# Linear attention beside a squared-ReLU MLP on one core: queries in the Strassen loop, a transposed second MLP product, and weight operands streamed from DRAM

## The chip, the cores and the metric

The kernel runs on one core of a Trainium2 chip. The metric is the device time of one execution in microseconds, from the first to the last thing that the core does. Before the change it is 423.73 us, the median of three runs (423.67 to 424.07).

## The reference

The input x has 2048 tokens of 512 numbers. All numbers are 32-bit floats. The output is x plus two branches that read the same normalised tokens:

```python
xn = layernorm(x)                                  # 2048 x 512
# branch A: linear attention, 32 heads of 16
q, k, v = split(xn @ wqkv)                         # wqkv 512 x 1536
phi = lambda t: where(t > 0, t + 1, exp(t)) + 1e-6
kv  = phi(k)^T @ v  (16 x 16 per head);  z = sum over tokens of phi(k)
o   = (phi(q) @ kv) / (phi(q) . z + 1e-6)
A   = o @ wo                                       # wo 512 x 512
# branch B: MLP
h   = relu(xn @ w1 + b1) ** 2                      # w1 512 x 1376
B   = h @ w2 + b2                                  # w2 1376 x 512
out = x + A + B
```

## The kernel before, in words

Tokens come in 16 tiles of 128 and four blocks of four tiles (512 tokens). `NF` = 11 chunks of 128 columns make up w1; the last has 96 and carries the bias b2 as an extra row, so `NP` = 5 pairs of whole chunks remain. Every large operand is kept as a high and a low part in a rounded 32-bit format (`split`, line 114: ScalarE copies the high part, VectorE subtracts it from the source for the low part). A product of two split operands is three passes (high·high, high·low, low·high; `three`, line 124), each a matmul with a 128x128 stationary operand and 512 columns moving.

The work goes in this order. First come the statistics and the normalisation. Then a loop over the 16 tiles (line 612 on) computes keys (`project`, line 329), their phi (`phi_k`, line 342) and `kx`, the product of phi(k) with the tokens (line 346, four accumulators). In that loop `pieces` (line 603) converts weights that are needed later. After it, `values` and `matrix` (lines 727 and 742) fold kv and wo into one 512x512 matrix m that is kept in SBUF.

The main loop `for n in range(2)` (line 750) takes two blocks at a time, t1 and t2. In it:

- `queries` (line 357) computes q of one tile with 12 matmuls and `phi`; `attention` (line 365) multiplies by z, sums over the 16 columns of a head, takes the reciprocal and scales; `regroup_q` and `attention_T` turn the result by DMA moves and VectorE transposes.
- The loop over `p` (line 869) computes the hidden columns of one pair of w1 chunks for both blocks by the Strassen-Winograd scheme: seven `product` calls (line 420) of six matmuls each instead of eight. The sums of w1 chunks (`chunk_sums`, line 656) and their parts (`chunk_split`) are made on chip in `aop`, right before they are used, and again for each n. The sums of tokens are in `T`.
- `mlp_2` (line 428) multiplies the hidden columns (stationary) with a chunk of w2 (moving, in `w2r`, made by `piece_2`, line 192): 12 matmuls for one chunk and four tiles. For t1 it runs inside the loop over p, for t2 after it (line 994 on), where `add_attention` (line 432) adds the attention product.
- The tokens-by-columns result gets x added by one VectorE instruction a tile (`add`, line 861) and leaves by one DMA a tile (`store`, line 865). The last tile is done in two halves of 256 columns (`end`).

Order and resources: this is a manual schedule; each engine runs its instructions in the order in which the program writes them. All DMAs are issued by the SP queue, in program order too: a DMA that must wait holds up those behind it. PSUM has two sets of four banks, `ps` and `acc`, which take turns. The instruction names in the profile are the tile names with numbers left out: `acc` for the second product, `b` for the Strassen products, `pk`, `pq` and `kx` for keys, queries and the token product.

## Time and profile before

| | before |
|---|---|
| median of three runs | 423.73 us |
| span of the profiled execution (first to last instruction) | 422.3 us |
| what lies around the span | 1.4 us |
| TensorE matmul, busy | 417.5 us (99%) |
| VectorE, busy | 298.8 us (71%) |
| ScalarE, busy | 248.4 us (59%) |
| GpSimd, busy | 28.7 us (7%) |
| bytes moved by DMA | 43.02 MB, mean 102 GB/s |
| granted TensorE clock | 1.00 all the way |

The profile is of one execution. It gives each engine's busy time, the chain of work that ended last, groups of like instructions with count and mean duration, and tables by stretches of time. Matmuls are pipelined, so the mean duration of one is longer than the distance between two. "PEld" is the loading of stationary operands, beside the matmuls.

### The profile page before, as it was taken

To read this page: it belongs to the slowest core of one execution; us is meant where nothing else is said; L and a number is where in the kernel's file an instruction comes from. 1 tells how busy PE (TensorE), PEld (TensorE's weight loads), DVE (VectorE), ACT (ScalarE), POOL (GpSimd) and SP (SyncE) were. 2 spreads that over 40 slices of the span, in tenths; PEclk is the share of its full clock that TensorE was granted. 3 is DMA by queue.
4 is the path that set the end of the run, shared out by engine and by line. 5 is a ranking of instruction groups with operands and counts; after the bars stand their busy time and mean duration, and the time that the engine had idled before them with its cause. 6 is when DMAs were issued, how large, how long until landed. Compare 5 with 4: busy or idle time off the path is not lost.

```text
span 422.3 us, 5369 instructions
## 1 busy us (share of the span) xinstructions
PE 417.5 (99%) x1868; PEld 345.2 (82%) x1868; DVE 298.8 (71%) x537; ACT 248.4 (59%) x441; POOL 28.7 (7%) x50
## 2 busy tenths in 40 slices
PE   8999999999999999999999999999999999999996
PEld 7788888888887888888888888888888888888885
DVE  6897788855668886777579376586977668577353
ACT  5766667644467777566467353666667665556240
POOL 2242222230000000000000000000000000000000
PEclk9999999999999999999999999999999999999999
DMA  7863437000412321646016752501120654024502
GB/s 236 281 168 83 107 102 223 25 0 2 112 50 58 93 72 54 185 87 177 0 54 203 185 201 76 144 0 50 51 75 25 200 98 152 1 87 95 162 0 99
DMA packets 42754, 43.02 MB, mean 102 GB/s; under 512 B 5828, under 2 KB 28612, under 8 KB 42472
## 3 DMA queue, kind: packets, MB, share of 16 engines
q1 hardware_dynamic: 42728, 42.69, 34.5%
q8 instruction: 14, 0.23, 0.3%
q14 instruction: 12, 0.10, 0.1%
HBM read 30.09 MB, written 6.29 MB: 86 GB/s over the span
## 4 chain that ended last, share of the span: by engine, by line
PE 99%; DVE 0%; issue 0%
PE acc L127 38%; PE b L424 23%; PE pk L332 10%; PE kx L351 10%; PE pq L332 10%; PE pz L127 1%; PE b L127 1%; PE warm L464 1%; PE pt L275 1%; PE pkv L733 1%; PE pm L127 1%; PE end L127 0%; DVE zb L439 0%; DVE res L863 0%; DVE eps L440 0%
## 5 line engine op out<-in xcount | busy, mean ns | idle before, releaser
L127 PE MATMUL acc<-w2r,s 128*128 128x512 f32 x498 | 116.6, 389 | 0.0
L127 PEld LDWEIGHTS acc<-w2r,s 128*128 128x128 f32 x498 | 93.5, 188 | 19.6
L424 PE MATMUL b<-T,aop 128*128 128x512 f32 x240 | 59.6, 389 | 0.0
L424 PEld LDWEIGHTS b<-T,aop 128*128 128x128 f32 x240 | 45.0, 188 | 9.4
L351 PE MATMUL kx<-pk,tok 128*128 128x512 f32 x192 | 47.0, 394 | 0.0
L351 PEld LDWEIGHTS kx<-pk,tok 128*128 128x128 f32 x192 | 35.5, 188 | 7.8 <-DVE pk L340 0.5
L127 PE MATMUL acc<-mh,aTsr 128*128 128x512 f32 x96 | 30.3, 390 | 0.0
L108 ACT ACTIVATE w2r<-r 128x512 fp32r<-128x512 f32 x32 | 20.0, 625 | 13.6 <-PE acc L127 11.3
L119 DVE TENSOR_TENSOR w2r<-r,w2r 128x512 fp32r<-128x512 f32 x32 | 21.9, 685 | 7.3 <-ACT w2r L108 7.2
L424 PE MATMUL b<-xs0h,aop 128*128 128x512 f32 x80 | 26.4, 391 | 0.0
L116 POOL TENSOR_TENSOR tok<-xp,tok 128x512 fp32r<-128x512 f32 x16 | 22.4, 1402 | 53.5 <-ACT tok L108 53.5
L116 DVE TENSOR_TENSOR s<-c,s 128x512 fp32r<-128x512 f32 x20 | 13.8, 692 | 16.7 <-ACT s L108 16.7
L327 DVE SCALAR_TENSOR_TENSOR q<-pq,q 128x512 f32<-128x512 f32 x16 | 11.0, 689 | 16.7 <-ACT q L325 16.7
L108 ACT ACTIVATE aop<-S 128x512 fp32r<-128x512 f32 x20 | 12.6, 629 | 14.7 <-DVE S L662 9.4
L127 PEld LDWEIGHTS acc<-mh,aTsr 128*128 128x128 f32 x96 | 18.0, 188 | 3.8
L863 DVE TENSOR_TENSOR res<-acc,res 128x512 f32<-128x512 f32 x16 | 11.0, 692 | 14.0 <-PE acc L127 13.9
L198 POOL MEMSET r<- 32x512 f32 x3 | 1.6, 522 | 278.3 <-DVE w2r L119 278.3
L323 ACT ACTIVATE q<-pq 128x512 f32<-128x512 f32 x16 | 9.5, 591 | 18.4 <-PE pq L332 18.4
L323 ACT ACTIVATE k<-pk 128x512 f32<-128x512 f32 x16 | 9.5, 594 | 17.0 <-PE pk L332 16.8
L127 PE MATMUL acc<-ml,aTsr 128*128 128x512 f32 x48 | 18.7, 390 | 0.0
L424 PEld LDWEIGHTS b<-xs0h,aop 128*128 128x128 f32 x80 | 15.0, 188 | 3.4 <-ACT rz L412 0.3
L424 PE MATMUL b<-xs0l,aop 128*128 128x512 f32 x40 | 15.6, 389 | 0.0
(188 smaller groups left out, 831.4 us busy)
## 6 DMA issues: line engine op xcount, KB each, us to landing
r<-in_B_w_dram SPq DMA_DIRECT2D x49, 256.0 KB, 3.2
res<-in_A_x_dram SPq DMA_DIRECT2D x8, 512.0 KB, 6.0
g<-q SPq DMA_DIRECT2D x64, 64.0 KB, 2.1
out_dram<-res SPq DMA_DIRECT2D x15, 256.0 KB, 2.0
x<-in_A_x_dram SPq DMA_DIRECT2D x5, 512.0 KB, 4.3
xTd<-t SPq DMA_DIRECT2D x8, 256.0 KB, 3.1
rq<-in_A_wqkv_dram SPq DMA_DIRECT2D x8, 256.0 KB, 5.8
xg<-xp SPq DMA_DIRECT2D x32, 64.0 KB, 2.0
```

The source lines that it names most:

```text
L108: nc.scalar.activation(o, i, AF.Copy, bias=bias)
L116: ENG[el].tensor_tensor(out=l, in0=src, in1=f32(h), op=OP.subtract)
L119: nc.vector.tensor_tensor(out=l, in0=src, in1=f32(h), op=OP.subtract)
L127: nc.tensor.matmul(ps, lhsT=a[u], rhs=b[v], start=first and n == 0, stop=last and n == 2)
L275: nc.tensor.transpose(p[:, at_j], xp[i][:, at_j], ident)
L323: nc.scalar.activation(p, ps, AF.Relu, scale=-1.0)
L327: nc.vector.scalar_tensor_tensor(p, ps, 0.0, p, op0=OP.max, op1=OP.add)
L332: nc.tensor.matmul(ps, lhsT=cols(i)[u][:, j, slot(i)], rhs=w[v][:, j, :], start=first and n == 0, stop=last and n == len(steps) - 1)
L351: nc.tensor.matmul(kxp[c], lhsT=tok[i][:, u, c * P:(c + 1) * P], rhs=pk[i][:, v], start=i == 0 and (u, v) == first, stop=i == NT - 1 and ( ...
L424: nc.tensor.matmul(ps, lhsT=a[u][:, j * P:(j + 1) * P], rhs=b[v][:, j, :], start=first and j == 0 and n == 0, stop=last and j == 1 and n == 2,
L464: nc.tensor.matmul(pw[:, :P], lhsT=zb[:, :P], rhs=zb[:, :P], start=True, stop=True)
L863: nc.vector.tensor_tensor(out=r[:, a:z], in0=ps, in1=r[:, a:z], op=OP.add)
```

## The change

The change rewrites the main loop.

- Queries no longer run tile by tile. The four chunks of wq become `NQ` = 2 pairs at the head of the Strassen loop, so the loop has `NK` = 7 pairs; a pair's outputs are transposed (columns on partitions). phi (`phi_1`) and the shares of a head (`shares`: one ScalarE activation with scale and bias, VectorE transposes, a reduction over 32-wide blocks, reciprocal, transpose back, scale) work on that form. `attention`, `regroup_q` and `attention_T` are gone.
- The second MLP product is transposed: the weights are stationary and the hidden columns move (`second`: six matmuls with two stationary 128-column halves and three passes into two banks). For the first two blocks (n = 0) it has as many matmuls as before; for the last two (n = 1) pairs of w2 chunks and the two blocks are multiplied with seven products (`combinations` makes the sums of hidden columns, `prepare_t` those of w2).
- Every stationary operand of the loop is a 256 KB block [128, 512] that is prepared once (`prepare_1`, `prepare_2`, `prepare_t`, `prepare_z`: load, sum, split into a staging tile, `spill` to DRAM in `wd1`, `wd2`, `wdz`) and read back when it is used: `fetch_ops` keeps eight slots filled in the order `order_of` gives; `used` frees a slot after its six matmuls and issues the next fetch. `m` goes to DRAM (`wdm`) and is prepared like a w2 chunk.
- A table `PLAN` says at which of six places of a pair a preparation step ("p"), a share step ("l"), a token sum ("s") or a combination ("c") is issued.
- Results are transposed, so each goes through a VectorE transpose and an addition to x (`add_turned`); x is loaded and the output stored in blocks of 32 partitions with rows of 64 numbers, 256 bytes (`out_blocks`, `load_res`, `store`): 32 loads and 32 stores of 128 KB.

The diff, cut to its core (n = 1 and the preparation of w2 look alike):

```diff
-    def mlp_2(acc, f, s, first=False):
-        for k in range(TB):
-            three(acc[k], [s[:, u, k * P:(k + 1) * P] for u in range(2)], w2s[f], first, False)
+    def fetch_ops():
+        while order and op_turn[1] < len(op_slots) and order[0] in ready:
+            key = order.pop(0)
+            t = op_slots[op_turn[0] % 8]
+            nc.sync.dma_start(f32(t), place_of(*key))
+            loaded.append((key, t))
+            op_turn[0] += 1
+            op_turn[1] += 1
+    def used(n=1):
+        op_turn[1] -= n
+        fetch_ops()
+    def product(ps, key, b, first=False, last=False):
+        a = op(*key)
+        for j in range(2):
+            for n, (u, v) in enumerate(PASSES):
+                nc.tensor.matmul(ps, lhsT=a[:, u * 256 + j * P:u * 256 + (j + 1) * P], rhs=b[v][:, j, :], ...)
+        used()
+    def second(ps, key, s, first=False, last=False):
+        a = op(*key)
+        for n, (u, v) in enumerate(ORDER):
+            for c in range(2):
+                nc.tensor.matmul(ps[c], lhsT=a[:, u * 256 + c * P:u * 256 + (c + 1) * P], rhs=s[:, v], ...)
+        used()
+    def ops_of(kind, k, i, src, el="dve"):
+        n = src.shape[1]
+        t = stage()[:, :n]
...
+        split(o[:, 0], o[:, 1], src, "act", el)
+        spill(kind, k, i, t)
+    def prepare_1(k, el="dve"):
...
+        return [lambda: ops_of("1", k, 0, ra, el), sums_12, sums_34, lambda: ops_of("1", k, 6, rb[:, 1:], el)]
+    def add_turned(r, c, src):
+        o = w512("o", "d", 2)
+        nc.vector.transpose(o, src)
+        at = r[:, :, c // 2].rearrange("p b (d c) -> p b c d", c=2)[:, :, c % 2]
+        nc.vector.tensor_tensor(out=at, in0=o.rearrange("p (b d) -> p b d", d=32), in1=at, op=OP.add)
+    PLAN = ((("s", "s", "p", "p", "p", "p"), ("p",) * 6, ("p",) * 6, *[("pl", "l", "p", "p", "pl", "pl")] * 4, ("", "l", "l")),
+            (("", "", "", "", "", ""), ("", "l", "", "p", "p", ""), *[("l", "l", "p", "l", "c", "l")] * 2,
+             *[("p", "l", "c", "p", "cl", "p")] * 3, ("l", "c", "c")))
-        for p in range(NP + 1):
+        for p in range(NK + 1):
...
+                product(A, ("1", p, 0), [x[:, :2] for x in x1], True)
...
+            if f_before:
+                add_product(p - 1, 0)
+            if p:
+                product(before, ("1", p - 1, 6), [T[4][:, u] for u in range(2)], False, True)
+                finish(p - 1, 1, before)
...
+            product(A, ("1", p, 3), [T[2][:, u] for u in range(2)])
+            copy("act", R[2], A, one)
+            hook(plan.pop(0))
+            product(C, ("1", p, 5), [x[:, 2:] for x in x2], False, True)
...
+            if f_before:
+                add_product(p - 1, 1)
...
+            product(A, ("1", p, 4), [T[3][:, u] for u in range(2)])
+            if n == 0 and p == 3:
+                for b in (t1 - 2, t2 - 2):
+                    nc.sync.dma_start(xT[b], xTd[b])
+            if p == NK - 1:
+                res = {t1: load_res(t1, "W0" if n else "r3")}
...
+        jobs += attentions([*V, *W], 2, True, False)
+        at_end(lambda: (add_to(o["m5"], W), turned_to(t2, 2, o["m5"]), store(res[t2], t2, 1)))
+        jobs += phase_jobs(V, 7, False, True)
+        at_end(lambda: (turned_to(t2, 0, V), store(res[t2], t2, 0)))
```

More of the change, by code (lines that the diff above doesn't have):

```diff
@@ L79, in w512 @@
         return work.tile([P, 512], F32, name=name, tag=tag, bufs=bufs)
-    turns = {"x": [0, 2], "pair": [0, 5]}
+    turns = {"x": [0, 2], "pair": [0, 5], "raw": [0, 4], "st": [0, 4]}
     def next_tag(of):
@@ L407, in hidden_2, with second_z, parts_of @@
+    def second_z(ps, cs, s, first=False, last=False):
+        a = [op("z", 0, 2 + u) for u in range(2)]
+        for n, (u, v) in enumerate(ORDER):
+            for b, c in zip(ps, cs):
+                nc.tensor.matmul(b, lhsT=a[u][:, c * P:(c + 1) * P], rhs=s[:, v],
+                                 start=first and n == 0, stop=last and n == 2, skip_group_check=True)
+        used(2)
+    def parts_of(name, src):
         s = pair(name)
-        split(s[:, 0], s[:, 1], r, "act", "dve")
+        split(s[:, 0], s[:, 1], src, "act", "dve")
@@ L1025 @@
[L1025 to L1045 removed]
+                finish(p - 1, 3, t5)
```

874 lines of the change are left out of this document (453 added, 421 removed).

## Prediction, written before the changed kernel ran

> **What bounds the kernel now.** First the page's head: busy shares, the slices and the DMA queue.
>
> ```profile
> span 422.3 us, 5369 instructions
> ...
> PE 417.5 (99%) x1868; PEld 345.2 (82%) x1868; DVE 298.8 (71%) x537; ACT 248.4 (59%) x441; POOL 28.7 (7%) x50
> ...
> DMA  7863437000412321646016752501120654024502
> GB/s 236 281 168 83 107 102 223 25 0 2 112 50 58 93 72 54 185 87 177 0 54 203 185 201 76 144 0 50 51 75 25 200 98 152 1 87 95 162 0 99
> ...
> q1 hardware_dynamic: 42728, 42.69, 34.5%
> ```
>
> TensorE is busy in 99%; the DMA engines only in 34.5%, in bursts. A busy PE may still be waiting inside its pipeline, so I read the distance between matmuls next: the chain that ended last, and one stretch of the main loop from the table of windows.
>
> ```profile
> PE 99%; DVE 0%; issue 0%
> ...
> 207.80 54.60 PE acc L127 x240
> ```
>
> ```profile
> 300.00:315.00 15.00, 15.00 (x68) 12.43 (x67) 11.71 (x22) 10.26 (x18) 0.00 (x0) 1.00 0.24 69
> ```
>
> The chain is one row of matmuls; 240 of them take 54.60 us, 0.227 us each, at clock 1.00. So the matmul count sets the time, and a 512-column matmul is worth 0.227 us. In a Strassen stage of 15.00 us VectorE works 11.71 and ScalarE 10.26 us: both have room, neither has much.
>
> **TensorE's part.** The queries were 16 x 12 = 192 matmuls; as two pairs for two block pairs they are 2 x 2 x 7 x 6 = 168. The second product of the last blocks was 10 chunks x 8 tiles x 3 = 240; with seven products it is 5 x 7 x 6 = 210. All else keeps its count. 54 matmuls go: 54 x 0.227 = **-12.3 us**, if none of the rest waits. What the change brings onto the other engines decides.
>
> **DMA.** Each block of 256 KB feeds six matmuls, so the loop must take 262 KB every 6 x 0.227 = 1.36 us, and the blocks must have been written before. By the code the kernel moves 117 MB instead of 42.7. What does a full DMA move?
>
> ```profile
> 3.00:6.00 3.00, 3.00 (x16) 3.00 (x16) 2.17 (x8) 1.07 (x5) 0.00 (x0) 1.00 1.00 346
> 71.00:74.00 3.00, 3.00 (x15) 2.46 (x15) 3.00 (x4) 2.05 (x4) 0.83 (x2) 1.00 0.93 311
> 220.00:225.00 5.00, 5.00 (x24) 4.13 (x23) 4.86 (x10) 1.38 (x3) 0.00 (x0) 1.00 0.90 345
> 266.50:269.00 2.50, 2.50 (x12) 2.07 (x12) 1.33 (x2) 1.73 (x3) 0.00 (x0) 1.00 0.97 252
> ```
>
> The last two columns are DMA share and GB/s. Loads in rows of 2 KB give 346 at a full share (and 311/0.93 = 334); a mix of an 8 KB-row load with 2 KB-row stores gives 345/0.90 = 383; loads of w1 columns, 512-byte rows, 252/0.97 = 260.
>
> n = 0 is where blocks are both made and used. Counting the SP queue's DMAs of the changed kernel between the end of pair 0 and the end of pair 5, in blocks of 262 KB: 47 operand fetches (7 + 7 + 11 + 11 + 11), 50 spilled, 15 raw w2, wo-product and bias rows, 6 of w1, 4 of m, 8 of xT: 130 blocks, 34.1 MB. Transfer time: the 6 blocks of w1 1.6 MB / 260 = 6.0 us; the other 32.5 MB 84.8 us at 383, 93.9 at 346. TensorE needs for these five pairs 47 x 1.36 + 12 x 0.227 (m) = 66.7 us. The excess is 24 to 33 us. It can't be put off, since the SP queue is one line: a fetch stands behind the spills issued before it. Only the look-ahead covers some: eight slots are 10.9 us, less the landing of one.
>
> ```profile
> r<-in_B_w_dram SPq DMA_DIRECT2D x49, 256.0 KB, 3.2
> ...
> out_dram<-res SPq DMA_DIRECT2D x15, 256.0 KB, 2.0
> ...
> out_dram<-res SPq DMA_DIRECT2D x2, 128.0 KB, 1.7
> ```
>
> A block lands in 3.2 us, so 10.9 - 3.2, about 8 us, is cover. The wait is 16 to 25 us. I take **+16**: the traffic is a mix of stores and loads, as in the row that gives 383. The low end for the range is 0, should stores and loads together run well over the 383 of this trace.
> The Trainium skill (HBM Reference, Access; DMA: Bandwidth & Descriptors, Bandwidth) has a core streaming alone at about 425 GB/s; no full stretch here reaches it. By that the 32.5 MB take 76.5 us and the wait is 8 us instead of 16.
>
> In the other stages the stream fits: pair 6 has 4.5 MB in 15 us, the n = 1 loop's full pairs 9 fetches, 4 spilled and 2 raw blocks, 3.9 MB in 12.3 us (320 GB/s).
>
> The residual loads are in 256-byte rows, which this trace doesn't have: 1 MB for each block, two blocks nearly at once at the end of each loop. Bounds: at the 260 of 512-byte rows 2.1 MB take 8 us, at half of it 16. Operands in hand and issued between them cover 13 x 1.36 = 17.7 us in n = 0, ten (13.6 us) in n = 1; with the fetches between (3.5 and 1.4 us) and 3.2 us of landing the wait is 0 to 5 and 0 to 7. I take **+3** together.
> The Trainium skill's DMA page (Specifications) puts the smallest transfer at line rate at 512 bytes; no row here is under it, and by that rule the half rate, 16 us, is the likelier end, which would make +3 into +12 (5 and 7).
>
> **VectorE and ScalarE.**
>
> ```profile
> L116 DVE TENSOR_TENSOR s<-c,s 128x512 fp32r<-128x512 f32 x20 | 13.8, 692 | 16.7 <-ACT s L108 16.7
> ...
> L371 DVE TENSOR_REDUCE den<-pz 128x32 f32<-128x512 f32 x16 | 11.0, 686 | 0.6
> ...
> L261 DVE STREAM_TRANSPOSE at<-g 128x512 f32<-128x512 f32 x16 | 10.5, 690 | 7.1 <-DMA g<-q 7.1
> ...
> L373 DVE RECIPROCAL den<-den 128x32 f32<-128x32 f32 x16 | 5.7, 353 | 0.6
> ...
> L662 DVE TENSOR_TENSOR S<-S,r 128x256 f32<-128x256 f32 x10 | 4.2, 425 | 0.3
> ```
>
> ```profile
> 8.70 0.68 DVE L487 TENSOR_TENSOR wkl<-rk,wkh 128x512 fp32r<-128x512 f32 x1
> 9.30 0.68 DVE L293 TENSOR_TENSOR xs1l<-pt,xs1h 128x512 fp32r<-128x512 f32 x1
> ```
>
> A 512-wide instruction takes 0.69 us, but the next can start 0.60 us later (8.70, 9.30). Those are the two ends. A full pair of n = 0 has 17 such, 5 of 256 and 2 reciprocals: 17 x 0.69 + 5 x 0.42 + 0.7 = 14.5 us in 15.0 (11 x 1.36): the DMA wait hides it. In n = 1 a full pair has 9 x 1.36 = 12.3 us of TensorE, and VectorE 16 x 0.69 + 6 x 0.42 + 0.35 = 13.9 us, 11.9 by the closer spacing; for the two heaviest pairs 0 to 3.2 us over. I take **+2**.
>
> At the end of that loop VectorE has ten instructions left (six sums of hidden columns among them) and then the low part for the first job: 11 x 0.60 to 0.69 = 6.6 to 7.6 us, while TensorE has two operands and four matmuls, 3.6 us: **+3**. Later, at three borders of the n = 1 sums, six VectorE instructions (3.6 to 4.1 us) and a split (0.69) stand before the third job's low part, which TensorE wants after the same 3.6 us: 0.7 to 1.2 each, **+2**.
> The short chain of a pair, from the A22 product over relu, square and high part on ScalarE to the second product, is three ScalarE instructions of 0.63 to 0.69 and has two operands (2.7 us) to hide in: nothing, at most 0.6 a pair if ScalarE is behind, 6 in all. A full pair of n = 0 gives ScalarE 18 instructions, 11.5 us of 15.
>
> **The tail.**
>
> ```profile
> 417.47 1.59 PE L127 MATMUL end<-w2r,s 128*128 128x256 f32 x12
> ...
> 419.10 0.42 DVE L863 TENSOR_TENSOR res<-end,res 128x256 f32<-128x256 f32 x1 [0.29 <-PE end L127]
> ```
>
> ```profile
> 36.61 10.11 SPq L257 DMA_DIRECT2D xg<-xp x16
> ```
>
> Now TensorE ends at 419.06 and the span at 422.3, 3.2 us later: half an addition and one small store. After the change both banks of the last sum end together: two transposes and two additions (4 x 0.60 + 0.1 = 2.5 us), then four stores, issued 0.63 us apart (10.11 us for 16), so the last 1.9 us after the first, then the 2.8 us that stand now behind the last addition, and 0 to 2 more for 256-byte rows. 7.2 to 9.2 us against 3.2: **+5**.
>
> **Sum.** 422.3 - 12.3 + 16 + 3 + 2 + 3 + 2 + 5 = 441.0; the 1.4 us around the span (423.73 less 422.3) make **442 us**, slower by 4%.
>
> **Rivals.**
> 1. *The transfers keep up*: stores and loads together pass the 383 and the waits shrink to what the look-ahead covers. Then -12.3, the tail +4 to +5, and 0 to 4 for VectorE: 415 to 421, faster. For it: stretches of a full DMA with mixed traffic are few here and short. Against it: it needs 34.1 MB in 66.7 + 8 us, 456 GB/s, over every row above. Chance 0.17.
> 2. *Partly*: 430 GB/s in the mix; the wait is 32.5/0.43 + 6.0 - 66.7 - 8 = 7 us, the rest at its low ends (+9): 423.7 - 12.3 + 16 = 427. Chance 0.15.
> 3. *The preparations come late as well*: in the full queue a raw row lands behind eight others (8 x 262 to 524 KB, 6 to 11 us), ScalarE, in order, waits for it at the split, and with it the copies that TensorE needs, so a fetch that has landed doesn't help. It decides as soon as a step is asked for less than such a time after its load was issued; a step is asked for every 2.5 to 3 us and at most three are held. One such wait of 2 to 4 us in each of five pairs: 452 to 462. Chance 0.22.
> 4. *The cut does not show*, because the second product gains nothing per matmul from going in two banks by turns: for 0.01 us more on 690 matmuls, +7. The present second product changes its stationary operand with every matmul too and runs at 0.227, so 0.02, together with no change at all.
>
> The forecast, 430 to 451, has 0.44. The range: rival 1 at its lower end and rival 3 at its upper: **415 to 462**, which leaves out some 0.15. Faster by over 0.2% 0.18, within 0.2% (about what a measurement can tell) 0.03, slower 0.79.
>
> **What the profile will show.** Right: 1722 matmuls of 512 columns at 0.227 where nothing waits; DMA slices of 9 tenths and 340 to 400 GB/s from the first pairs to the fifth of n = 0, with TensorE waiting there for operand blocks and nearly nowhere else; a gap of about 3 us after the n = 1 loop; 7 to 9 us from the last matmul to the end. Wrong: DMA shares below 0.9 in n = 0 while TensorE waits (then the queue's order or a split is the wait, not the rate); rates over 420 there; waits in n = 1 that sum to more than 15 us.

## The result, and the profile after

The changed kernel takes **515.39 us** (median of four runs, 511.4 to 518.54) against 423.7 for the kernel before: ratio 1.216, 95% interval [1.210, 1.222]. Slower was foretold, but by 4%, not by 22%, and 515 lies far outside the range of 415 to 462. The profiled execution took 518.5 us, the longest of the four; its span is 516.4.

The page's head of the changed kernel: the span, TensorE's busy time, the slices of the granted clock and of the DMA engines, the queue, and the chain that ended last by engine.

```profile
span 516.4 us, 5845 instructions
...
PE 443.2 (86%) x1808; PEld 346.0 (67%) x1808; DVE 331.0 (64%) x551; ACT 255.6 (49%) x438; POOL 28.1 (5%) x48
...
PEclk9999899999888897999879999989989898799998
DMA  7834556556899899999976877776447749956853
...
q1 hardware_dynamic: 96868, 117.09, 73.0%
...
DVE 31%; PE 28%; ACT 16%; DMA 12%; issue 7%; SPq 4%; DVEq 0%; ACTq 0%
```

The chain was 99% TensorE; now VectorE leads with 31%, although VectorE is busy in only 64% of the span. No engine is full. The matmuls became fewer and TensorE's busy time grew from 417.5 to 443.2 us: some of them ran at nearly half rate (in the timeline of pair 5 of n = 1 six take 2.90 us at 403.83 and 1.52 at 390.26). The DMA is at 8 or 9 tenths throughout in slices 11 to 20 alone (12.9 us each): the n = 0 loop.

So I went by stage. A **pair** is here what lies between the first products of two turns of the loop over p. Pairs 1 to 5 of n = 0 take 95.9 us together (first products at 124.9 and 220.8), where their 294 matmuls at 0.227 us need 66.7. Pairs 0 to 5 of n = 1 take 98.2 us (309.8 to 408.0) instead of 69.5 (306 matmuls). These two stretches hold 58 of the 104 us between 515.4 and 411.4 (the kernel before, less 54 matmuls).

The rest is spread. Counted in the same way in the profiled execution (3 us longer than the median), 22.6 us are lost in pair 6 of n = 1 and the jobs behind that loop, which are the products that remain after it (408.0 to 508.2), 12.7 in pair 6 of n = 0 and the jobs behind it (7.9 and 9.7 in noprep1 and bare1 below, which are the same kernel up to there), 6.5 in the loop over keys (it ends at 102.7, before at 96.2), 5.0 from the last matmul to the end and 2.4 in pair 0 of n = 0. The table of windows of the changed kernel, one row for a pair (busy us of PE, PEld, DVE, ACT, POOL, then clock, DMA share, GB/s): pairs 2 and 4 of n = 0, then 1, 3, 4 and 5 of n = 1, and last pair 6 of n = 1 up to the first job.

```profile
142.60:160.60 18.00, 12.95 (x44) 9.30 (x43) 9.97 (x18) 12.09 (x22) 0.00 (x0) 0.82 1.02 377
...
181.70:203.70 22.00, 18.14 (x67) 13.96 (x66) 14.89 (x26) 11.46 (x19) 0.52 (x1) 0.84 1.02 394
325.00:334.50 9.50, 9.50 (x43) 7.88 (x42) 6.34 (x10) 5.50 (x10) 0.00 (x0) 1.00 0.76 217
350.10:368.50 18.40, 13.87 (x55) 9.82 (x56) 11.72 (x21) 10.73 (x17) 0.00 (x0) 1.00 0.50 172
368.50:387.50 19.00, 14.80 (x55) 10.77 (x54) 12.99 (x23) 10.73 (x18) 0.00 (x0) 0.91 0.54 180
387.50:408.00 20.50, 15.03 (x56) 10.79 (x56) 12.95 (x23) 10.71 (x18) 0.00 (x0) 0.92 0.72 239
408.00:436.60 28.60, 18.09 (x67) 12.78 (x65) 18.64 (x32) 15.94 (x27) 0.00 (x0) 0.94 0.73 200
```

In n = 0 the DMA is full, as foretold. In n = 1 it is not (0.50 to 0.76), and there the loss is as large: a full pair of 12.3 us of matmuls takes 18.4 to 20.5, with VectorE at 11.7 to 13.0 and ScalarE under 11. Pair 6 has 66 matmuls, 15.0 us, and takes 28.6. What does TensorE wait for? The table of waits of the changed kernel (us in total, times, longest):

```profile
ACT st L108 <- DVE t L281: 20.6, 8, 4.4
PE b L503 <- ACT rr L108: 16.9, 12, 3.9
PE b L503 <- DVE rr L990: 14.3, 8, 3.5
PE b L503 <- ACT rf L108: 9.7, 4, 4.2
ACT st L108 <- DMA raws<-in_B_w_dram: 5.4, 3, 2.1
PE b L503 <- DMA ops<-wd: 2.7, 3, 1.2
PE acc L521 <- DMA ops<-wd: 1.0, 1, 1.0
```

It hardly waits for operand blocks (`ops`). It waits for its banks: for ScalarE to copy one out, for VectorE to add to one. Within pairs 1 to 5 of n = 0 TensorE's waits are 15.5 us for banks (9.7 for copies, 5.8 for additions) and 2.1 for operand blocks, and within pairs 0 to 5 of n = 1 they are 17.5 for banks and 1.2 for ScalarE's and VectorE's parts. The rest of what is lost in the two stretches, some 11 and 10 us, is matmuls that ran slower than 0.227 us.

The timeline of pair 5 of n = 1 shows how such a copy comes late. TensorE's order in a pair is A11, A12, S1 (blocks 0, 1, 2), a second product, A22 of the pair before, S2, S4, a second product, S3. Line 108 copies a bank, 990 and 998 add a bank, 540 is the relu, 281 a sum of w2 chunks for a preparation.

```profile
392.02 0.41 DVE L281 TENSOR_TENSOR t<-raws,t 128x256 f32<-128x256 f32 x1
392.47 0.66 ACT L108 ACTIVATE st<-t 128x512 fp32r<-128x512 f32 x1 [3.71 <-DVE t L281]
...
393.77 0.68 DVE L990 TENSOR_TENSOR rr<-b,rr 128x512 f32<-128x512 f32 x1
394.49 0.72 ACT L540 ACTIVATE rr<-rr,b1s 128x512 f32<-128x512 f32 x1 [1.36 <-DVE rr L990]
...
395.78 0.58 ACT L108 ACTIVATE rr<-b 128x512 f32<-128x512 f32 x1
396.39 0.69 DVE L998 TENSOR_TENSOR rr<-b,rr 128x512 f32<-128x512 f32 x1 [1.94 <-ACT rr L108]
397.12 0.72 ACT L540 ACTIVATE rr<-rr,b1s 128x512 f32<-128x512 f32 x1 [0.76 <-DVE rr L998]
...
400.72 0.66 ACT L108 ACTIVATE st<-t 128x512 fp32r<-128x512 f32 x1 [1.55 <-DVE t L281]
401.28 0.58 ACT L108 ACTIVATE rr<-b 128x512 f32<-128x512 f32 x1
401.92 0.50 PE L503 MATMUL b<-xs1h,ops 128*128 128x512 f32 x1 [3.85 <-ACT rr L108]
```

Read it backwards. S4 starts at 401.92, after the copy of S1's bank at 401.28; S1 had ended near 391.7. ScalarE could have copied at once, but in its order there stand first: a preparation's high part that waits 3.71 us for VectorE's sums (which stood behind a combination and a share), a relu that waits for VectorE's addition, the copy of A11, a relu that waits for the next addition, and a second high part that waits for sums. Each engine waits for the other in turn, and neither is full.

The end of the changed kernel, from TensorE's timeline (start, us; in brackets the idle time before and who ended it): the first two jobs after the n = 1 loop, and the last product, with the last addition on VectorE.

```profile
436.62 1.52 PE L521 MATMUL Y<-s,ops 128*128 128x512 f32 x4 [3.59 <-ACT s L108]
440.45 6.54 PE L521 MATMUL Y<-s,ops 128*128 128x512 f32 x20 [2.30 <-DVE s L116]
...
504.66 3.51 PE L521 MATMUL V<-s,ops 128*128 128x512 f32 x14 [0.82 <-DVE s L116]
...
510.09 0.69 DVE L872 TENSOR_TENSOR res<-o,res 128x512 f32<-128x512 f32 x1
```

From the last matmul (508.2) to the end it is 8.2 us, 5.0 more than before: that term was right.

### The profile page after: what moved, and what is told of

It is laid out like the page before. It is cut to its first block, busy times and chain, and to the rows that moved or that the text cites. A ratio compares the mean times of both kernels' runs of the same rounds, so it can differ in the third digit from the quotient of the medians.

```text
span 516.4 us, 5845 instructions
## 1 busy us (share of the span) xinstructions
PE 443.2 (86%) x1808; PEld 346.0 (67%) x1808; DVE 331.0 (64%) x551; ACT 255.6 (49%) x438; POOL 28.1 (5%) x48
## 4 chain that ended last, share of the span: by engine, by line
DVE 31%; PE 28%; ACT 16%; DMA 12%; issue 7%; SPq 4%; DVEq 0%; ACTq 0%
PE acc L521 13%; DMA raws<-in_B_w_dram 5%; DVE st L116 4%; DMA ops<-wd 4%; PE b L503 4%; PE Y L521 4%; ACT st L108 4%; ACT rr L540 2%; ACT s L108 2%; DVE s L116 2%; SPq L345 2%; PE V L521 2%; DVE o L870 2%; DVE st L301 1%; ACT rr L543 1%
## 5 line engine op out<-in xcount | busy, mean ns | idle before, releaser
L521 PE MATMUL acc<-s,ops 128*128 128x512 f32 x480 | 124.4, 414 | 6.5 <-ACT s L108 3.6
L521 PEld LDWEIGHTS acc<-s,ops 128*128 128x128 f32 x480 | 95.4, 201 | 32.9 <-ACT s L108 6.7
L503 PE MATMUL b<-T,ops 128*128 128x512 f32 x336 | 91.4, 414 | 19.4 <-DVE rr L990 14.3
L503 PEld LDWEIGHTS b<-T,ops 128*128 128x128 f32 x336 | 65.0, 198 | 40.9 <-DVE rr L990 17.6
L116 DVE TENSOR_TENSOR s<-rr,s 128x512 fp32r<-128x512 f32 x46 | 29.7, 686 | 24.8 <-ACT s L108 24.8
L503 PE MATMUL b<-xs1h,ops 128*128 128x512 f32 x56 | 22.9, 450 | 24.4 <-ACT rr L108 14.9
L108 ACT ACTIVATE s<-rr 128x512 fp32r<-128x512 f32 x46 | 27.4, 628 | 28.6 <-PE acc L521 15.8
L503 PE MATMUL b<-xs0h,ops 128*128 128x512 f32 x112 | 37.0, 392 | 0.1
L116 DVE TENSOR_TENSOR st<-raws,st 128x512 fp32r<-128x512 f32 (+1 forms) x30 | 21.9, 736 | 12.8 <-ACT st L108 10.9
L521 PE MATMUL Y<-s,ops 128*128 128x512 f32 x84 | 22.8, 422 | 6.7 <-ACT s L108 4.4
L108 ACT ACTIVATE rr<-b 128x512 f32<-128x512 f32 x27 | 15.6, 582 | 14.6 <-PE b L503 14.5
L540 ACT ACTIVATE rr<-rr,b1s 128x512 f32<-128x512 f32 x15 | 10.9, 724 | 23.7 <-DVE rr L990 10.4
L540 ACT ACTIVATE rf<-rf,b1s 128x512 f32<-128x512 f32 x10 | 7.2, 723 | 23.2 <-DVE rf L990 15.7
```

What stands on the lines that cost most here:

```text
L108: nc.scalar.activation(o, i, AF.Copy, bias=bias)
L116: ENG[el].tensor_tensor(out=l, in0=src, in1=f32(h), op=OP.subtract)
L503: nc.tensor.matmul(ps, lhsT=a[:, u * 256 + j * P:u * 256 + (j + 1) * P], rhs=b[v][:, j, :], start=first and j == 0 and n == 0, stop=last a ...
L521: nc.tensor.matmul(ps[c], lhsT=a[:, u * 256 + c * P:u * 256 + (c + 1) * P], rhs=s[:, v], start=first and n == 0, stop=last and n == 2, ski ...
L540: nc.scalar.activation(o, i, AF.Relu, bias=b1s[:, f:f + 1])
```

## The experiments

Three explanations were set against each other. **Rate**: the transfers hold TensorE in n = 0 (the prediction's +16). **Hand-over**: copies and additions that free banks stand behind preparations, shares and combinations in the order of ScalarE and VectorE. **Clock**: a waiting TensorE is throttled, and half-rate matmuls multiply whatever the waits cost.

All whole times are medians of four runs (of three for noprep1); the stretches are those of one profiled execution, from first product to first product, and the first row is worked out from 0.227 us a matmul.

| run | whole, us | ratio to before, 95% | n = 0, pairs 1 to 5 | n = 1, pairs 0 to 5 |
|---|---|---|---|---|
| matmuls alone | | | 66.7 | 69.5 |
| changed kernel | 515.4 | 1.210 to 1.222 | 95.9 | 98.2 |
| nofetch | 507.4 | 1.195 to 1.199 | 92.1 | 95.9 |
| noprep1 | 489.8 | 1.151 to 1.159 | 95.6 | 79.4 |
| early | 503.8 | 1.186 to 1.193 | 94.9 | 91.6 |
| wide | 513.8 | 1.207 to 1.216 | 94.9 | 98.6 |
| noprep0 | 481.7 | 1.134 to 1.139 | 66.8 | 98.8 |
| bare1 | 478.6 | 1.125 to 1.133 | 96.6 | 71.0 |
| skewearly | 494.6 | 1.165 to 1.169 | 91.3 | 87.3 |
| sepool | 493.7 | 1.163 to 1.168 | 93.9 | 85.8 |
| sepsums | 484.3 | 1.141 to 1.145 | 88.9 | 80.1 |
| sepoolm | 492.5 | 1.160 to 1.165 | 96.7 | 86.5 |
| fill | 515.7 | 1.212 to 1.219 | 96.4 | 96.4 |
| traffic0 | 501.9 | 1.181 to 1.187 | 82.5 | 98.1 |
| sepsnf | 473.3 | 1.115 to 1.122 | 81.8 | 80.5 |
| bareboth | 445.1 | 1.048 to 1.053 | 66.8 | 71.0 |

### Without the fetches (nofetch)

```diff
-            nc.sync.dma_start(f32(t), place_of(*key))
+            if op_turn[0] < 8:
+                nc.sync.dma_start(f32(t), place_of(*key))
```

> The changed kernel, but only the first eight operand blocks are fetched from DRAM; every later product reads whatever lies in the eight slots. Leaves out some 197 fetches of 262 KB (about 52 MB of 117), so the output is not the reference's; all copies, sums, splits and spills stay. Rate theory (the term of +16 in the prediction: 34.1 MB at 383 GB/s hold TensorE in pairs 1 to 5 of n = 0): 47 of the 130 blocks go, 21.8 MB are left, which fit into the 66.7 us that TensorE needs, so the n = 0 loop falls from 134 us to 98 to 105 and the whole to 480 to 488; n = 1 stays at 131. Hand-over theory (TensorE waits for copies and additions that free its banks, and these stand in ScalarE's and VectorE's order behind preparations and shares): the raw rows land sooner, so n = 0 gains 5 to 15 us, it stays above 115, and n = 1 gains under 5; the whole 495 to 512.

It took 8 us off the whole and 3.8 off pairs 1 to 5 of n = 0. Pair 3 of that loop, in the windows of this run:

```profile
160.70:180.40 19.70, 17.06 (x67) 13.17 (x66) 12.61 (x22) 11.96 (x21) 0.00 (x0) 0.91 0.60 211
```

No operand can be late here and the DMA share is down to 0.60, yet the pair lasts 19.7 us for 15 of matmuls. The rate is not what held it in the changed kernel.

### Without preparations in n = 1 (noprep1), and without shares too (bare1)

```diff
-            todo = [lambda k=k: prepare_t(k) for k in range(NP)]
+            todo = []
...
-                queues["l"] += shares(R[i], 2 * k + i % 2)
+                queues["l"] += shares(R[i], 2 * k + i % 2) if n == 0 else []
```

The first edit alone is noprep1 (the fetches of sums read plain blocks); both are bare1.

> The changed kernel without the five preparations of second-product sums in the n = 1 loop: per chunk pair four 256-wide sums, two splits (two 512-wide instructions on ScalarE, two on VectorE), two loads and one or two spills fewer; the seven products read the plain blocks of n = 0 instead of the sums, so the output is not the reference's. Rate theory: n = 1 has DMA shares of 0.50 to 0.72 and isn't bounded by it, so its loop stays within 4 us of 131. Hand-over theory: what stands between a product and the copy that frees its bank gets shorter by about 1.4 us on ScalarE and 3 us on VectorE in each of five or six pairs, and the waits for sums at the splits (20.6 us over the run) go for n = 1: its loop falls from 131 to 100 to 115 us, the whole to 485 to 500, and the granted clock in that loop rises above 0.95.

> The run without preparations in n = 1, and there without the steps of the shares as well (denominators and quotients of the four query tiles of each pair, 10 instructions on VectorE, 2 on ScalarE for each tile pair): attention goes in unnormalised for these blocks, and the output is not the reference's. Pairs 0 to 5 of n = 1 took 98.2 us in the changed kernel and 79.4 without preparations; their matmuls alone take 69.5. Hand-over theory, in its form that what stands between matters: 70 to 75 us, the whole 480 to 488. In the form that the chain of a pair alone sets it: 78 to 80, no change by the shares, since they are over in the first pairs with a second product.

The n = 1 stretch went from 98.2 to 79.4 and then to 71.0, as the hand-over theory has it in the form that what stands between matters. The windows of bare1, pair 3:

```profile
341.40:353.60 12.20, 12.20 (x55) 10.13 (x54) 4.75 (x7) 9.00 (x15) 0.00 (x0) 1.00 0.69 194
```

The pair is now as long as its matmuls, PE busy in all of it, at clock 1.00. Pair 6, 28.6 us up to the first job in the changed kernel, takes 18.9 here. The copies, additions, relus, squares, splits and combinations of a pair are all still there: by themselves they hold nothing up. VectorE does 4.7 us in a pair of 12.2 where it did 11.7 to 13.0 in one of 18.4 to 20.5. A busy share by itself is no limit: in the window of the kernel before that the prediction shows, VectorE worked 11.71 and ScalarE 10.26 of 15.00 us, and TensorE did not wait. bare1 takes away work and, with it, what stands ahead of copies and additions in the order of the two engines; it does not part the two.

### Without preparations in n = 0 (noprep0)

```diff
-    todo += [lambda: prepare_1(NQ + 1)]
-    for k in range(NP - 2):
-        todo += [lambda k=k: prepare_2(k), lambda k=k: prepare_1(NQ + 2 + k)]
...
+    ready.update(("1", k, i) for k in range(NQ + 1, NK) for i in range(7))
```

> The changed kernel without any preparation in the n = 0 loop: the blocks of the later block pairs and the plain second-product blocks are not made (their loads, sums, splits and spills go, some 50 spilled and 25 raw blocks), and every fetch of one reads a block that was made in the loop over keys, so the output is not the reference's. All fetches, copies, relus, shares, and n = 1 with its own preparations stay. Hand-over theory (preparation steps stand ahead of the copies and additions that free TensorE's banks): pairs 1 to 5 of n = 0, 95.9 us in the changed kernel against 66.8 of matmuls, fall to 68 to 78; n = 1 stays; the whole 488 to 500. Rival, the chain of a pair alone (copy, addition, relu, square, split follow one another on two engines whatever stands between): they stay above 85. Rate theory: as the first, since two thirds of the traffic go; that the run without fetches kept 92.1 us there speaks against it already.

Pairs 1 to 5 took 66.8 us, the matmuls alone; this and the whole lie a little under what was expected (68 and 488). The window of pair 3 of this run:

```profile
146.70:161.70 15.00, 15.00 (x68) 12.43 (x67) 8.22 (x13) 8.61 (x14) 0.00 (x0) 1.00 0.70 192
```

This run takes away both the engines' work and its transfers, so it does not tell the two apart; traffic0 and sepsnf below do.

### The same work in another order (early, skewearly)

In early, the copies of A11's and S1's banks are issued ahead of the steps that wait for an addition:

```diff
             if p:
                 nc.vector.tensor_tensor(out=t5, in0=before, in1=t5, op=OP.add)
-                finish(p - 1, 3, t5)
             if p < NK:
                 copy("act", c11, A, one)
+            if p:
+                finish(p - 1, 3, t5)
...
-                finish(p, 0, c11)
-                hook(plan.pop(0))
                 product(C, ("1", p, 2), [T[1][:, u] for u in range(2)], True)
                 copy("act", t5, C, one)
+                finish(p, 0, c11)
+                hook(plan.pop(0))
```

> The changed kernel with the same work, another order on ScalarE and VectorE: the copy of the A11 product and that of the S1 product are issued before the relu and the splits that wait for an addition, in both loops. Rate theory: no transfer changes, n = 0 stays at 134 us within 4, n = 1 gains under 5. Hand-over theory: TensorE's 17 us of waits for the copy after the S1 product (rows of PE b waiting for ACT rr) and most of the 9.7 for ACT rf go, and with them gaps long enough to lower the clock: 15 to 30 us less in all, at least 8 of them in n = 1; the whole 485 to 500.

The whole fell by 11.6 us, less than expected; n = 0 by 1 us, n = 1 by 6.6. The waits of this run say why:

```profile
PE b L503 <- DVE rr L990: 17.8, 7, 4.4
ACT rr L108 <- PE b L503: 20.6, 5, 14.3
PE acc L521 <- ACT s L108: 13.2, 6, 3.3
```

The row of `b` waiting for the copy into `rr` fell from 16.9 to 2.8 us. In its place the second product (`acc`) waits 13.2 us, where it was 3.6, for ScalarE's high part of the hidden columns, which now stands behind, and the waits for the addition of line 990 grew from 14.3 to 17.8. ScalarE waits for the bank, no longer the bank for ScalarE. The queue is as long as it was; another of its customers is last.

In skewearly the two engines also no longer wait for each other inside a preparation step:

```diff
-            ops_of("1", k, 2, o, el)
+            later.append(ops_of("1", k, 2, o, el, True))   # (high, low) of these sums
...
+            last = later.pop(0) if later else None
+            if last:
+                last[0]()
             if held:
                 held.pop(0)()
+            if last:
+                last[1]()
```

> All work, correct output. The copies of the A11 and S1 products early, and, new, each preparation step of sums one step apart: the high part of the last step's sums on ScalarE, then this step's sums on VectorE, then the last step's low part, so that neither engine waits for the other inside a step (rows of ACT st waiting for DVE t, sa and sb: 43.8 us in the changed kernel, of DVE st waiting for ACT st 28.4). Hand-over theory: those rows fall to under 15 and under 10, pairs 1 to 5 of n = 0 from 94.9 (early copies alone) to 80 to 90, pairs 0 to 5 of n = 1 from 91.6 to 78 to 86, the whole from 503.8 to 478 to 494. If it is the engines' sum of work and not the order that sets the time: no more than 3 us below early copies alone.

ScalarE's waits for sums (43.8 us) left the table's first 60 rows, VectorE's for high parts fell from 28.4 to 19.1, and the whole came to 494.6, just above the expected band, as did both stretches. Together the two edits give 21 us back without any work removed; 71 stay.

### Idling or work (fill), and the clock by itself (micro)

```diff
+            if p >= NQ + 2:
+                for _ in range(10):
+                    nc.tensor.matmul(acc[0], lhsT=zr, rhs=x1[0][:, 0, :], start=False, stop=False, ...)
             product(C, ("1", p, 5), [x[:, 2:] for x in x2], False, True)
```

> The changed kernel with ten matmuls more (of a zero stationary operand, so they add nothing to the sum) in each of pairs 4, 5 and 6 of both loops, before the product that waits longest: 60 matmuls, 13.6 us of TensorE by 0.227, as work in place of idling. Correct output. Clock theory (a gap of 2.7 us or more costs 1.4 to 2.7 us of matmuls at half rate behind it): the gaps of 2.8 to 3.9 us shrink to under 2, the granted clock in these pairs goes from 0.84 to 0.92 to above 0.96, and the added matmuls cost nothing or less than nothing: pairs 4 and 5 of n = 1 from 19.0 and 20.4 us to 17 to 19, the whole 506 to 515. If the gaps did not lower the clock, or the chain of the other engines sets the pair's time whatever the clock: pair times unchanged, and the whole within 3 us of 515.4. If gaps aren't there to be filled: up to 13.6 us more.

60 matmuls more, 13.6 us of TensorE, and the time is the same: 515.7. Pairs 4 and 5 of n = 1 in this run:

```profile
365.30:383.20 17.90, 15.78 (x66) 11.70 (x64) 12.56 (x22) 9.60 (x16) 0.00 (x0) 1.00 0.51 170
383.20:403.50 20.30, 17.29 (x65) 12.67 (x64) 12.99 (x24) 10.53 (x18) 0.00 (x0) 0.92 0.72 240
```

The clock rose to 1.00 in one and stayed 0.92 in the other; the pairs take 17.9 and 20.3 us instead of 19.0 and 20.5. So the other engines set most of a pair's time whatever TensorE does meanwhile, and most of the half-rate matmuls ran in time that was lost anyway. The clock theory falls as the main cause. A small share may still be the clock's: where it rose to 1.00, in pair 4 of each loop, the pair got 1.1 us (n = 1) and 1.2 us (n = 0, 22.0 to 20.8) shorter although it had 2.3 us more of matmuls.

The clock itself is real. In micro it is measured alone:

```python
def row(k, n):
    for m in range(n):
        nc.tensor.matmul(banks[k % 2], lhsT=a[:, :P], rhs=s, start=m == 0, stop=m == n - 1)
def gap(k, g):
    nc.scalar.activation(s, banks[k % 2], AF.Copy, scale=0.02, bias=0.05)
    for _ in range(g - 1):
        nc.scalar.activation(s, s.bitcast(F32), AF.Copy)
```

> Not the kernel's computation: one stationary operand, rows of 60 matmuls of 512 columns, and between them a chain of 1 to 8, 10 and 12 dependent ScalarE copies, on which the next row waits; then four stretches of ten short rows of 6 matmuls with 1, 2, 3 or 4 copies between, each followed by 60 matmuls. The output is a copy of the last bank. Clock theory (in the changed kernel matmuls came 0.42 to 0.48 us apart for about 3 us after waits of 2.85 to 4.2 us): rows after short gaps run at 0.227 from the first matmul; from some gap between 2 and 5 us on, the first 7 or so matmuls of a row run at 0.45; the short rows with the longest gaps run at 0.45 throughout. If gaps don't matter and slow matmuls come from something else (operands, banks, power): 0.227 in every row.

Rows of 60 in TensorE's timeline of micro, the idle time ahead of each in brackets:

```profile
59.31 13.90 PE L65 MATMUL ps<-s,a 128*128 128x512 f32 x60 [2.07 <-ACT s L70]
75.94 15.27 PE L65 MATMUL ps<-s,a 128*128 128x512 f32 x60 [2.73 <-ACT s L70]
...
114.19 16.55 PE L65 MATMUL ps<-s,a 128*128 128x512 f32 x60 [4.05 <-ACT s L70]
```

After one gap of 2.07 us (as of 0.75 and 1.41) a row takes 13.90 us (0.23 each), after one of 2.73 us 1.4 more, after 4.05 us 2.65 more; gaps of 4.71 to 8.02 us cost 1.8 to 2.5. Short rows of six, the first with 1.41 us between, the others with 2.07:

```profile
283.43 1.65 PE L65 MATMUL ps<-s,a 128*128 128x512 f32 x6 [1.41 <-ACT s L70]
...
328.51 2.93 PE L65 MATMUL ps<-s,a 128*128 128x512 f32 x6 [2.07 <-ACT s L70]
```

All ten rows at 1.41 us run at full rate, nearly all at 2.07 at half: 2.93 us for six.

### Preparations moved to GpSimd (sepool, sepsums, sepoolm)

```diff
-    todo += [lambda: prepare_1(NQ + 1)]
+    todo += [lambda: prepare_1(NQ + 1, "pool")]      # sepool: low parts on GpSimd
...
-            nc.vector.tensor_tensor(out=o, in0=x, in1=y, op=op)
+            ENG[el].tensor_tensor(out=o, in0=x, in1=y, op=op)      # sepsums: sums too
```

All three stand on skewearly.

> The run with early copies and preparations one step apart, and now the low part of every preparation step of the two loops on GpSimd in place of VectorE (GpSimd does nothing there so far; the same form took it 1.47 us in the loop over keys, VectorE 0.69 to 0.79). All work, correct output. Hand-over theory: VectorE loses four instructions of 0.7 us in a full pair of n = 0 and two in n = 1, and no longer waits for ScalarE's high parts; pairs 1 to 5 of n = 0 go from 91.3 us to 78 to 86, pairs 0 to 5 of n = 1 from 87.3 to 77 to 83, the whole from 494.6 to 478 to 488. Rival: blocks come later by the slower engine, or VectorE gets slower beside it; then TensorE's rows of waits for operand blocks grow by what is won, and the whole stays within 3 us of 494.6 or above it.

> As the run with the low parts on GpSimd, and the sums of the preparations there too, so that VectorE has nothing of the preparations of the two loops and GpSimd all but the high parts. All work, correct output. Hand-over theory: VectorE's order now holds only what the pair itself needs, as in the runs without preparations, but ScalarE still has one high part a step, which now waits for GpSimd: n = 0 pairs 1 to 5 70 to 80 us, n = 1 pairs 0 to 5 73 to 80, the whole 468 to 482. Rival: a step on GpSimd takes 3 us or more (two sums, one low part), as long as the time between two steps; ScalarE, in order, waits for the sums and the blocks come late: 490 or more.

sepool gained nothing (493.7): the rival had it. VectorE has fewer instructions, but those with two operands in SBUF became slower. The same sums of w2 chunks in skewearly, by form (count, then busy us and mean ns):

```profile
L292 DVE TENSOR_TENSOR t<-raws,t 128x256 f32<-128x256 f32 x10 | 4.2, 420 | 0.5 <-DMA raws<-in_B_w_dram 0.3
```

and in sepool:

```profile
L292 DVE TENSOR_TENSOR t<-raws,t 128x256 f32<-128x256 f32 x10 | 7.4, 740 | 0.5 <-DMA raws<-in_B_w_dram 0.4
```

With the sums gone from VectorE as well, sepsums reached 484.3, near its band; n = 1 fell to 80.1, but n = 0 stayed at 88.9, far over the 70 to 80 expected, with a DMA share of 1.00 to 1.04 in pairs 2 to 5. So something else was close behind in n = 0.

> As the run with the low parts on GpSimd, and in the loop over keys the moves that turn the tokens are put into the SP queue ahead of that turn's preparations and spills. In the changed kernel that loop ends at 102.7 us against 96.2 before, with TensorE waiting 2.63 us at 57 for a transposed tile whose moves stood behind spills. If that order is the cause, the first product of n = 0 starts 2 to 5 us sooner than in the run with the low parts on GpSimd, and the rest is as there. If the loop is longer because VectorE and ScalarE have more preparation in it, it starts within 1 us of that.

```diff
+        move(8 if i >= NPE - 1 else 16)      # sepoolm
         pieces(PIECES[i])
...
-        move(8 if i >= NPE - 1 else 16)
```

In sepoolm the first product of n = 0 came at 106.4 us instead of sepool's 109.1, as expected of the SP queue's order; the whole fell by 1.2 us only, and pairs 1 to 5 of n = 0 took 96.7 instead of 93.9. The 2.7 us rest on one profiled execution of each, and such a time differs between executions of the same code: the loop over keys ended at 102.3 us in sepsums and at 100.9 in sepsnf, which are the same up to there. The rest of the 6.5 us by which that loop got longer was not traced.

### Transfers alone and engines alone in n = 0 (traffic0, sepsnf)

In traffic0 a preparation step still loads and spills, but computes nothing:

```diff
-        split(o[:, 0], o[:, 1], src, "act", el)
+        if not bare:
+            split(o[:, 0], o[:, 1], src, "act", el)
         spill(kind, k, i, t)
```

> The changed kernel with every load, spill and fetch of the n = 0 loop, but without the sums and splits of its preparation steps on ScalarE and VectorE: the spills store what lies in the stage, so the output is not the reference's. n = 1 has its own preparations in full. If the transfers are a limit of their own (the prediction's 6.0 + 84.8 us for 34.1 MB, less 8 us of look-ahead): pairs 1 to 5 of n = 0 take 80 to 91 us, TensorE waits there for operand blocks, and the whole is 498 to 512. If only the engines' order held them: 67 to 72 us, as without preparations, and the whole 480 to 490.

sepsnf is sepsums with the edit of nofetch.

> The run with the sums and low parts of preparations on GpSimd, and only the first eight operand blocks fetched (the output is not the reference's). There pairs 1 to 5 of n = 0 took 88.9 us with a full DMA. If transfers are the second limit: 68 to 78 us here, and the whole 464 to 474. If ScalarE's and VectorE's order still holds that loop: above 83, and the whole within 6 us of 484.3. n = 1 stays near 80 for pairs 0 to 5 in both cases.

Pairs 1 to 5 take 82.5 us with the transfers alone. The windows of pairs 2 and 3 of traffic0:

```profile
137.30:147.40 10.10, 9.72 (x44) 7.73 (x42) 4.50 (x7) 7.02 (x12) 0.00 (x0) 1.00 1.04 410
147.40:169.40 22.00, 16.38 (x67) 12.07 (x68) 9.42 (x15) 8.36 (x13) 0.00 (x0) 1.00 1.05 402
```

and two of TensorE's waits in its timeline:

```profile
164.99 3.00 PE L525 MATMUL acc<-s,ops 128*128 128x512 f32 x12 [1.50 <-DMA ops<-wd]
...
185.33 5.46 PE L525 MATMUL acc<-s,ops 128*128 128x512 f32 x12 [4.87 <-DMA ops<-wd]
```

Here TensorE does wait for operand blocks, 10.9 us in these pairs, and for nothing else. 82.5 less the 66.8 of noprep0 is 15.7 us, the prediction's +16; but 4.8 of it are no waits, but matmuls that took longer than 0.227 us, which the prediction did not count. So the transfers are a limit of their own at 82.5, and the engines' order another at 92.1 (nofetch); the kernel with both takes 95.9. sepsnf, GpSimd's preparations without fetches, gave 81.8 where 88.9 had been: between the two bands, so it decides only that the transfers held 7 us of that run and that the engines' order still holds about 15.

### What is left (bareboth), and the rows of 256 bytes (wide)

bareboth joins the edits of noprep0 and bare1.

> No preparations in either loop (fetches read blocks made in the loop over keys) and no shares in n = 1; the output is not the reference's. If the losses of the two loops are independent, the gains add up: 515.4 - 33.7 - 36.8 = 445, and the rest over the kernel before less its 54 matmuls (411.4) lies in the loop over keys, the jobs behind each loop and the tail. If something that both loops share were behind (the clock, the queue), the sum would not hold: 455 or more, or under 438.

445.1, as the two gains add up. So the losses of the two loops are independent as far as this shows, and even with no preparation at all the kernel is 21 us slower than before. The window over the end of its n = 1 loop and the first jobs, where the residual rows are loaded:

```profile
344.50:375.00 30.50, 24.98 (x97) 19.07 (x95) 14.16 (x23) 15.32 (x27) 0.00 (x0) 0.89 0.99 205
```

TensorE works 25.0 of these 30.5 us, at clock 0.89. Since the two stretches of pairs are within 1.5 us of their matmuls, what remains (445.1 against 411.4) lies elsewhere. Counted as above, it is 6.1 us in the loop over keys, 2.4 in pair 0 of n = 0, 5.9 in pair 6 of n = 0 and the jobs behind it, 12.6 in pair 6 of n = 1 and the jobs behind it, and 4.9 in the tail. Pair 6 of n = 1 takes 18.9 us up to the first job where it took 28.6: what held the other pairs held this one too.

```diff
-        rows = w[t * BT:(t + 1) * BT, :].rearrange("(b t) n -> t b n", t=32)
+        rows = w[t * BT:(t + 1) * BT, :].rearrange("(g r p) n -> g p r n", g=NJ, r=4)
```

That is wide.

> The changed kernel with the residual rows loaded, and the results stored, in rows of 2 KB in place of 256 bytes: equal bytes, number of transfers and issues, another layout, so the output is not the reference's. Prices the residual term of the prediction (+3, +12 by the rule on the smallest transfer). If 256-byte rows move at half rate: the last pair of n = 1 (15.4 us) and the end of n = 0 lose 3 to 8 us together, the tail 1 to 2: the whole 503 to 511. If they cost what other rows cost: within 2 us of the changed kernel. The hand-over theory says nothing of it, except that a chain that waits for other things anyway takes back part of what is saved.

513.8 against 515.4, intervals that overlap: nothing that these runs can tell of the whole, though the time behind the last matmul was 7.3 us instead of 8.2. Eight residual loads leave the SP queue in 4.95 us with rows of 2 KB and in 6.62 with rows of 256 bytes, but around them the DMA moves hardly more: 242 GB/s at a share of 0.96 in 420 to 430 us of wide, 224 at 1.02 in 427 to 437 of the changed kernel. The packets in the two traces show more. In the changed kernel, from 427 to 445 us, 1.95 MB in packets of 256 bytes took 12.5 us of the 16 DMA engines (155 GB/s), and 1.79 MB in packets of 2 KB beside them 6.0 us (301 GB/s). In wide, from 420 to 438 us, where all 4.07 MB are in packets of 2 KB, they took 17.2 us (237 GB/s). So the residual loads did run at about half the rate of the others, but with rows of 2 KB most of that stays; what makes them slow is not shown.

## Why the prediction was wrong

Point by point, by its own steps:

- **TensorE, -12.3: right.** Where nothing waits, pairs take what the count at 0.227 us gives (noprep0, bare1), 66.8 where the prediction had 66.7.
- **DMA, +16: near in size by luck in part, wrong in place.** The transfers are worth 15.7 us when they are alone, of which 10.9 are the waits that the step is about. But the step took them for the only limit ("the DMA wait hides" VectorE's 14.5 us in a pair of 15). They aren't: with 29 us lost in these pairs TensorE waited only some 6 us for operand blocks in the whole run (2.7 + 1.0 in the rows above, 2.6 more for `wdz`), and without fetches 25 us of the loss are still there. The Trainium skill has 425 GB/s for a core that streams alone (HBM Reference, Specifications (TRN2)). No run reached it: the highest of the 40 slices of any page is 415 (traffic0).
- **VectorE in n = 1, +2: this is the step that failed.** The prediction put VectorE's work in a pair, 11.9 to 13.9 us, beside the 12.3 us of the matmuls and charged the difference. VectorE's work was indeed 12 to 13 us. But a pair is not over when VectorE has had 12 us of work: its instructions must come between ScalarE's and TensorE's, in order, and it was idle for 6 to 7.6 us of each of pairs 3 to 5 while those that needed it waited. Measured: 28.7 us in pairs 0 to 5, of which preparations are 18.8 (noprep1) and shares 8.4 (bare1). Those runs take away work; by order alone, with all the work left, 10.9 of them came back (skewearly). How the other 17.8 divide between the order and the amount of work was not tried.
- **The short chain, "nothing, at most 6 in all": the same fault.** The chain had its cover only if ScalarE and VectorE are free when it comes to them. TensorE waited 40.9 us for the copies and additions of its banks (16.9 + 14.3 + 9.7), which the prediction did not list. It followed the second product's inputs, not the banks that A22 and S4 go into.
- **Drain at the end of the n = 1 loop, +3:** 3.59 + 2.30 = 5.9 us of waits there, right in kind, half in size. **Borders, +2:** waits of 0.37 to 0.82 us where 0.7 to 1.2 were foretold. **Tail, +5:** 5.0, right.
- **What the sum had too little or nothing for.** Pair 6 of n = 1 with the jobs behind it lost 22.6 us where drain and borders gave it 5; 13.7 of them are in pair 6 itself, by the same fault as in the pairs before it (3.9 stay in bareboth). Pair 6 of n = 0 and its jobs lost 12.7, for which there was only a part of the residual term. The loop over keys and pair 0 lost 8.9, and there the sum had nothing ("All else keeps its count"). Against the sum these places are some 36 us over, pairs 0 to 5 of n = 1 are 27 over and pairs 1 to 5 of n = 0 are 13: together the 76 us between 442 and the 518.5 of the profiled execution.
- **256-byte rows, +3:** within what can't be told (wide). Behind the residual loads TensorE waited 2.6 us for operand blocks (those of `wdz`) after the n = 0 loop and nothing after the n = 1 loop. By the Trainium skill's rule on the smallest transfer (DMA: Bandwidth & Descriptors, Specifications) the prediction had 12 as its other estimate. The loads' rate was near that half (155 against 301 GB/s), but rows of 2 KB won little, and 12 us of waits did not come.
- **Rival 3** named the right engine and the right reason, an in-order ScalarE with copies behind a wait, and gave it 0.22. It put the wait at raw rows that land late (5.4 us in the table of waits) and only where the queue is full; the waits were for VectorE's sums (20.6 us for w2 alone) and additions, and those sums are made in n = 1 alone, where the queue is not full. So its 462 left out the larger place.
- Of what would show it wrong, one thing came: waits in n = 1 that sum to more than 15 us (18.7 in pairs 0 to 5). Of what would show it right, one failed: in n = 0 TensorE was to wait for operand blocks and nearly nowhere else, and it waited 2.1 us for them and 15.5 for banks. The DMA share in n = 0 was as foretold (0.89 to 1.02 in pairs 1 to 5), which shows that a full queue is no proof of a wait for it.

What stays open: how the 95.9 us of n = 0 come from limits of 82.5 and 92.1 in detail, what more than the SP queue's order lengthens the loop over keys, and what of the jobs behind the two loops is lost to what.

## What to carry to other kernels

Engines that hand a result back and forth in order can't be costed by adding up their work: list for each bank or buffer the instruction that frees it and everything that stands ahead of it on its engine, and charge the waits inside that row. Here VectorE kept up with 4.7 us of work in a pair of 12.2, and no longer with 12 to 13 in one of 12.3; in the kernel before it kept up with 11.7 in 15.0, so the busy share alone does not tell. Where two limits lie side by side, take each away alone before believing either, for removing the lower one shows almost nothing.

## What the runs showed of the hardware

- A granted clock at half came after a single gap of 2.73 us (0.50 from 75.94 to 78.80 us of micro), not of 2.07, and with rows of six matmuls (1.65 us) after nearly every gap of 2.07 us, never of 1.41. The Trainium skill (TensorE: Matmul & The Clock Gate, What's actually happening) has half the pulses after an idle window of about 3.4 us; the half clock agrees (six matmuls take 2.93 us against 1.65), the length was less here.
- GpSimd beside VectorE made VectorE's sums of two SBUF operands 1.76 times as long (420 to 740 ns), while its additions with a PSUM operand kept their 0.67 us. The Trainium skill (SBUF — State Buffer, section "SBUF: two separate sides") says of just this pair that one holds the shared port and the other waits; the runs agree.
- A full DMA with mixed stores and loads moved 402 GB/s at a share of 1.05, 383 at a share of 1, the figure of the kernel before.
